# A two-layer kernel on one core: the second layer's up product by seven block products over pairs of batches

## The chip, the core and the metric

One core of a Trainium2 chip. TensorE (PE) does matrix products into PSUM, eight banks of 128 x 512 fp32; VectorE (DVE) and ScalarE (ACT) read PSUM and SBUF and work element by element; GpSimd (POOL) and SyncE (SP) here only issue DMA transfers, each on a queue of its own. The metric is device time of one execution in microseconds; lower is better.

## The reference

```python
attn_out = _attn_ref(x, state)            # x (4, 8, 512, 64), state (4, 8, 32, 64)
x = attn_out.transpose(0, 2, 1, 3).reshape(4 * 544, 512)
h = x @ w_in;  g = h - tanh(h);          x = g @ w_out     # 512 -> 2048 -> 512
h = x @ w2_in; g = h * tanh(softplus(h)); out = g @ w2_out  # 512 -> 2048 -> 512
```

Attention gives per batch 512 rows read by x and 32 read by the states: 4 x 512 rows and 128 state rows. Two layers follow, each an up product (512 to 2048), an elementwise function and a down product (2048 to 512). The weights come as float64.

## The kernel before

Every fp32 product is made of three matmuls on pairs of fp32r tiles (`mm3p`): high x high, high x low, low x high. `split` makes such a pair: a copy to fp32r on ACT or DVE gives the high part, a subtraction on DVE the low part. Weights arrive as float64 by SP, and `conv_steps` turns them into fp32 (two ACT instructions and one on DVE, two after the second layer's table is loaded).

The first layer runs batch after batch (0, 1, 2, state rows, 3), each in 16 steps of 128 columns of d_ff (the state rows in 4 steps). A step has an up product of 6 matmuls, `elem1` (tanh on ACT, subtraction on DVE, a split) and, three steps later (`LA = 3`), a down product of 12 matmuls into four banks. Other work is attached to steps (`at`): attention of the next batch, `sw` (state times weight), and `late_conv`, which converts the second layer's weights along a ramp, and goes on in the second layer's first 13 steps.

The second layer cuts the 17 chunks of 128 rows into blocks of 4, 4, 4, 3 and 2 chunks (`BLOCKS`). `up_2` makes 128 columns of d_ff for a block: 4 k tiles x 3 matmuls, 512, 384 or 256 columns wide; Mish on ACT; a split. `down_2`, three steps later, adds 3 matmuls of 512 columns per chunk, in PSUM over all 16 steps; only the last step is copied out and stored. All split weights of the second layer stay in SBUF.

Buffers are 91 slots of 128 x 512 fp32, handed out oldest first (`get`, `put`); some 1024-wide buffers are given out as halves. In the second layer ACT and DVE work in program order (`Pinned`); in the first, the scheduler chooses it by priority. All instructions on PE, ACT and DVE are recorded under one line, 59, so rows are told apart by their tiles: `h` is an up product, `acc` a down product, `ath`/`swh` first-layer operands, `yh`/`yl` second-layer inputs, `gh`/`gl` the split result of the elementwise function, `wh`/`wl` split weights.

Of the kernel before, what the change touches and what calls it, by code (L numbers as in the profile page):

```python
# [9 lines left out]
F32 = mybir.dt.float32  # L10
# [10 lines left out]
REBIAS = 2.0 ** -112  # L21
NEGATIVE = 2.0 ** 32
PLAIN = 3
YSPARE = 4

# [46 lines left out]
def attention_moe_kernel(  # L72
# [25 lines left out]
        )  # L98

    TE, AC, V = (Pinned(e, order) for e in (nc.tensor, nc.scalar, nc.vector))  # L100
    misc = ctx.enter_context(tc.tile_pool(name="misc", bufs=1))
    small = ctx.enter_context(tc.tile_pool(name="small", bufs=2))
    stage = ctx.enter_context(tc.tile_pool(name="stage", bufs=3))
# [9 lines left out]
    def get(name, dtype=F32, newest=False):  # L113
        if halves and dtype == F32:
            return halves.popleft()
        i = free.pop() if newest else free.popleft()
        return Unit(slots.tile([128, 512], dtype, tag=f"k{i}", name=name), i)

    def put(*units):
        for u in units:  # L120
            if u.slot is None:
                halves.append(u)
            else:
                free.append(u.slot)
# [101 lines left out]
        )  # L226
        return h, l

    W1I, W1O, W2I, W2O = {}, {}, {}, {}

    def conv_w1i(c, k):
        W1I[c, k] = conv32(("w1i", c, k))
# [318 lines left out]
    def acc_bank(i, tags=("a0", "a1", "a2", "a3")):  # L551
        return psum.tile([128, 512], F32, tag=tags[i % len(tags)], name=f"acc{i}")
# [75 lines left out]
        put(u)  # L628
        Y["s"] = y

    chunks = [(b, r) for b in range(3) for r in range(4)] + [("s", 0)] + [(3, r) for r in range(4)]
    blocks = []
    for z in BLOCKS:
        blocks.append(chunks[:z])
        chunks = chunks[z:]

    def y_piece(n):
        ch = blocks[n]
        runs = []
        for i, (b, r) in enumerate(ch):  # L640
            if runs and runs[-1][0] == b:
                runs[-1][3] += 128
            else:
                runs.append([b, r * 128, i * 128, 128])
        k = len(YB.setdefault(n, []))
        yh, yl = get("yh", F32R), get("yl", F32R)
        for b, s0, d0, w in runs:
            src = Y["s"].t[:, k * 128:(k + 1) * 128] if b == "s" else Y[b, k].t[:, s0:s0 + w]
            AC.activation(out=yh.t[:, d0:d0 + w], in_=src, func=ACTF.Copy)
            V.tensor_tensor(  # L650
                out=yl.t[:, d0:d0 + w], in0=src, in1=yh.t[:, d0:d0 + w].bitcast(F32),
                op=ALU.subtract,
            )
        YB[n].append((yh, yl))
        for b, r in ch:
            if b != "s" and r == 3:
                put(Y.pop((b, k)))

    def y_block(n, spare=0):
        if n < len(blocks):  # L660
            while len(YB.get(n, [])) < KD and len(free) >= 2 + spare:
                y_piece(n)
                if spare:
                    break

    ACCT = ["a0", "a1", "a2", "a3"]
    HT = ["s1", "s0", "h0", "h1"]
    acc_n = [0]
    def up_2(n, t):
        N = 128 * len(blocks[n])  # L670
        h = h_bank(HT)[:, :N]
        c, f = t // 4, (t % 4) * 128
        for k in range(KD):
            wh, wl = W2I[c, k]
            yh, yl = YB[n][k]
            mm3p(
                h, wh.t[:, f:f + 128], wl.t[:, f:f + 128], yh.t[:, :N], yl.t[:, :N],
                k == 0, k == KD - 1,
            )
        if t == NT - 1:  # L680
            for p in YB.pop(n):
                put(*p)
        g = get("g")
        AC.activation(out=g.t[:, :N], in_=h, func=ACTF.Mish)
        G["2", n, t] = split(g.t[:, :N], N, "g")
        put(g)

    def down_2(n, t):
        ch = blocks[n]
        if t == 0:  # L690
            ACC["2", n] = []
            for _ in ch:
                ACC["2", n].append(acc_bank(acc_n[0], ACCT))
                acc_n[0] += 1
        gh, gl = G.pop(("2", n, t))
        wh, wl = W2O[(t,)]
        for i, (b, r) in enumerate(ch):
            s = slice(i * 128, (i + 1) * 128)
            acc = ACC["2", n][i]
            if t == NT - 1 and n == len(blocks) - 1 and i == len(ch) - 1:  # L700
                o = get("o")
                rows_out = out[b * T:b * T + S, :].rearrange("(p r) d -> p r d", r=4)[:, r, :]
                for c0, parts in ((0, (256,)), (256, (128, 128))):
                    c1 = c0 + 256
                    mm3p(
                        acc[:, c0:c1], gh.t[:, s], gl.t[:, s], wh.t[:, c0:c1], wl.t[:, c0:c1],
                        False, True, skip_group_check=c0 > 0,
                    )
                    for e, m in enumerate(parts):
                        a = slice(c0 + e * m, c0 + (e + 1) * m)  # L710
                        evac(o.t[:, a], acc[:, a], e)
                    nc.sync.dma_start(out=rows_out[:, c0:c1], in_=o.t[:, c0:c1])
                put(o)
                continue
            mm3p(acc, gh.t[:, s], gl.t[:, s], wh.t, wl.t, t == 0, t == NT - 1)
            if t == NT - 1:
                o = get("o")
                evac(o.t, acc, i)
                if b == "s":
                    for bb in range(B):  # L720
                        nc.sync.dma_start(
                            out=out[bb * T + S:(bb + 1) * T, :], in_=o.t[bb * NS:(bb + 1) * NS, :]
                        )
                else:
                    nc.sync.dma_start(
                        out=out[b * T:b * T + S, :].rearrange("(p r) d -> p r d", r=4)[:, r, :],
                        in_=o.t,
                    )
                put(o)
        put(gh, gl)  # L730


    wi = [
        (("w1i", c, k), cols(w1i, c, k) if c else ftile(w1i, k)) for c in range(4) for k in range(KD)
# [3 lines left out]
        pending.append((("w1o", t), rows(w1o, t)))  # L738
        pending.extend(wi[5 + t:6 + t])
    for c in range(4):  # L740
        for k in range(KD):
            pending.append((("w2i", c, k), cols(w2i, c, k)))
    for t in range(NT):
        pending.append((("w2o", t), rows(w2o, t)))

    side = {}

# [21 lines left out]
    for n in range(len(blocks)):  # L769
        start["2", n] = len(seq)  # L770
        seq += [("2", n, t) for t in range(NT)]

    for s in range(16):
        at(s, lambda s=s: conv_w1o(s))
# [24 lines left out]
    at(start["2"] - 4, lambda: y_block(0))  # L799
    late = [(W2I, ("w2i", i // 4, i % 4)) for i in range(16)]  # L800
    late += [(W2O, ("w2o", i)) for i in range(16)]
    ramp = [
        (start["s"] - 16, 0), (start["s"], 6), (start[3], 10), (start["2"], 25),
        (start["2"] + 13, len(late)),
    ]
    done = [0]

    def late_conv(i):
        for (s0, n0), (s1, n1) in zip(ramp, ramp[1:]):
            if s0 <= i < s1:  # L810
                goal = n0 + (n1 - n0) * (i + 1 - s0) / (s1 - s0)
                while done[0] < goal and len(free) >= (RESERVE if i < start["2"] else 5):
                    conv_split(*late[done[0]])
                    done[0] += 1

    def load_state(g):
# [81 lines left out]
    at(4, lambda: state_t(1, st[1]))  # L898
    banks[2:] = []

    def widen():
        for t in wide:
            put(*(Unit(t[:, h * 512:(h + 1) * 512], None) for h in range(2)))

    at(start[1], widen)
# [1 line left out]
    def up(q):  # L907
        if q[0] == "x":
            up_x(q[1], q[2])
        elif q[0] == "s":  # L910
            up_s(q[1])
        else:
            if q[2] == 0:
                if q[1] == 0:
                    pre = nc.scalar.preload_act_table_set("mish").ins
                    signed[0] = False
                    order(pre, last[0])
                    AC.last, V.last = pre, None
                    AC.floor = V.floor = None
                    AC.on = V.on = True  # L920
                y_block(q[1])
            up_2(*q[1:])

    def down(q):
        if q[0] == "x":
            down_x(q[1], q[2])
        elif q[0] == "s":
            down_s(q[1])
        else:
            down_2(q[1], q[2])  # L930

    def ahead(i):
        return LA if i < len(seq) else 0

    low = 0
    for i in range(len(seq) + 1):
        marks.append([e.recent for e in engines])
        q = seq[i] if i < len(seq) else None
        if q:
            up(q)  # L940
            if q[0] == "2" and q[2] >= NT - 6:
                y_block(q[1] + 1, YSPARE)
        for f in side.pop(i, []):
            f()
        while low < len(seq) and low <= i - ahead(i):
            down(seq[low])
            low += 1
        pinned = AC.on, V.on
        AC.on = V.on = False
        late_conv(i)  # L950
        AC.on, V.on = pinned


# [31 lines left out]
```

## Time and profile before

| | |
|---|---|
| median of 3 runs | 744.0 us (743.06 to 744.3) |
| the profiled execution | 743.11 us, span 741.3 us |
| PE busy | 726.9 us (98%), 4147 matmuls |
| DVE busy | 304.1 us (41%), 533 instructions |
| ACT busy | 332.6 us (45%), 612 instructions |
| POOL busy | 6.6 us (1%) |
| granted clock of PE | 1.00 throughout (2.4 GHz), 0.97 in the last 21 us |
| DMA | 43.1 MB, mean 58 GB/s |

The first layer's last batch begins near 285 us, and the second layer's first up product is issued at 355.3 us. A row of the timeline gives start, duration, engine, line, operation, output <- inputs and count; matmuls overlap, so the time of one is read from the distance of their starts. A table by stage gives busy time and number of instructions per engine.

### The profile page before, as it was taken

Reading aid. Unit: us, or ns where it says so; the run is one execution under the profiler, and the core shown is the slowest. Engines: PE = TensorE matmul, PEld = TensorE weight load, DVE = VectorE, ACT = ScalarE, POOL = GpSimd, SP = SyncE. Lnnn points to the kernel's source line nnn. Section 1 sums busy time; section 2 is a strip of 40 time slices with the busy share of each in tenths; the row PEclk is TensorE's granted clock in tenths of the full one; section 3 lists DMA queues with packets and bytes.
Section 4 is the critical chain, followed back from the end, with each engine's and each line's share of the span. In section 5 each row is a group of like instructions: output and inputs, shape, how many; then the busy total and the mean of one; then the engine's idle time right before and its main releaser. Section 6 shows DMA issues by size and latency. Waiting matters only on the chain.

```text
span 741.3 us, 10004 instructions
## 1 busy us (share of the span) xinstructions
PE 726.9 (98%) x4147; PEld 591.4 (80%) x4147; DVE 304.1 (41%) x533; ACT 332.6 (45%) x612; POOL 6.6 (1%) x14
## 2 busy tenths in 40 slices
PE   8899999999999999999999999999999999999997
PEld 6467877788777898778888888888888888998996
DVE  5899654844456443787633222111221111111111
ACT  6998544544554443787744333122231223223322
POOL 0000010001000000000000000000000000000000
PEclk9999999999999999999999999999999999999999
DMA  9984110003110110453400001000010000100100
GB/s 291 331 301 142 57 57 1 1 2 100 43 29 1 58 57 1 142 171 114 142 28 1 1 0 57 1 0 1 1 57 1 0 1 1 57 0 1 43 1 28
DMA packets 17308, 43.10 MB, mean 58 GB/s; under 512 B 2672, under 2 KB 7024, under 8 KB 17264
## 3 DMA queue, kind: packets, MB, share of 16 engines
q1 hardware_dynamic: 16624, 40.38, 16.3%
q0 software_dynamic: 640, 2.10, 1.0%
q8 instruction: 32, 0.52, 0.3%
q14 instruction: 12, 0.10, 0.1%
HBM read 38.01 MB, written 4.46 MB: 57 GB/s over the span
## 4 chain that ended last, share of the span: by engine, by line
PE 91%; ACT 6%; DVE 2%; DMA 1%; issue 0%; SPq 0%; ACTq 0%
PE acc L59 47%; PE h L59 37%; PE swp L59 2%; ACT w L59 2%; ACT r L59 2%; PE srd L59 1%; PE xtp L59 1%; ACT swh L59 1%; DMA x<-in_x_dram 1%; ACT t L59 1%; PE sct L59 1%; PE atp L59 1%; PE e2p L59 1%; DVE swl L59 0%; PE sc L59 0%
## 5 line engine op out<-in xcount | busy, mean ns | idle before, releaser
L59 DVE TENSOR_TENSOR gl<-wide,gh 128x512 fp32r<-128x512 f32 (+2 forms) x74 | 44.8, 605 | 198.3 <-ACT gh L59 198.3
L59 ACT ACTIVATE wide<-h 128x512 f32<-128x512 f32 (+2 forms) x74 | 39.0, 527 | 187.4 <-PE h L59 182.9
L59 PE MATMUL h<-yh,wl 128*128 128x512 f32 (+2 forms) x320 | 114.4, 358 | 0.0
L59 PE MATMUL h<-yl,wh 128*128 128x512 f32 (+2 forms) x320 | 114.3, 357 | 0.0
L59 PE MATMUL h<-yh,wh 128*128 128x512 f32 (+2 forms) x320 | 114.3, 357 | 0.0
L59 PE MATMUL acc<-wh,gh 128*128 128x512 f32 x289 | 112.7, 390 | 0.6 <-ACT wide L59 0.6
L59 PE MATMUL acc<-wl,gh 128*128 128x512 f32 x289 | 112.7, 390 | 0.0
L59 PE MATMUL acc<-wh,gl 128*128 128x512 f32 x289 | 112.5, 389 | 0.0
L59 PE MATMUL acc<-gh,wh 128*128 128x512 f32 x244 | 99.1, 406 | 0.0
L59 PE MATMUL acc<-gl,wh 128*128 128x512 f32 x244 | 95.4, 391 | 0.0
L59 PE MATMUL acc<-gh,wl 128*128 128x512 f32 x244 | 95.4, 391 | 0.0
L59 PEld LDWEIGHTS h<-yl,wh 128*128 128x128 f32 x320 | 60.2, 188 | 8.9 <-DVE yl L59 0.2
L59 PEld LDWEIGHTS h<-yh,wh 128*128 128x128 f32 x320 | 60.3, 188 | 8.9
L59 PEld LDWEIGHTS h<-yh,wl 128*128 128x128 f32 x320 | 60.3, 188 | 7.5
L59 PEld LDWEIGHTS acc<-wh,gh 128*128 128x128 f32 x289 | 54.3, 188 | 11.9 <-ACT t L59 0.8
L59 PEld LDWEIGHTS acc<-wh,gl 128*128 128x128 f32 x289 | 54.2, 188 | 11.4
L59 PEld LDWEIGHTS acc<-wl,gh 128*128 128x128 f32 x289 | 54.3, 188 | 10.2
L59 PEld LDWEIGHTS acc<-gh,wh 128*128 128x128 f32 x244 | 45.8, 188 | 17.2 <-issue 5.6
L59 DVE TENSOR_TENSOR gl<-g,gh 128x512 fp32r<-128x512 f32 x24 | 16.6, 692 | 94.3 <-ACT gh L59 94.3
L59 PEld LDWEIGHTS acc<-gh,wl 128*128 128x128 f32 x244 | 45.8, 188 | 9.9
L59 PE MATMUL h<-ath,swh 128*128 128x512 f32 x128 | 51.4, 402 | 1.8 <-DVE t L59 1.6
L59 PEld LDWEIGHTS acc<-gl,wh 128*128 128x128 f32 x244 | 45.9, 188 | 9.1 <-issue 0.8
(123 smaller groups left out, 925.6 us busy)
## 6 DMA issues: line engine op xcount, KB each, us to landing
st<-in_moe_w_in_dram SPq DMA_DIRECT2D x27, 512.0 KB, 4.6
st<-in_moe_w_out_dram SPq DMA_DIRECT2D x22, 512.0 KB, 3.4
wide<-in_moe_w_out_dram SPq DMA_DIRECT2D x10, 512.0 KB, 5.1
out_dram<-wide SPq DMA_DIRECT2D x11, 256.0 KB, 2.1
wide<-in_moe_w_in_dram SPq DMA_DIRECT2D x5, 512.0 KB, 6.4
x<-in_x_dram SPq DMA_DIRECT2D x8, 256.0 KB, 5.7
x<-in_x_dram POOLq DMA_DIRECT2D x6, 256.0 KB, 3.2
out_dram<-o SPq DMA_DIRECT2D x4, 256.0 KB, 2.3
```

Source lines behind the costliest of these rows:

```text
L59: i = fn(*args, **kw)
```

## The change

The up product of the second layer is computed for two batches at a time. The 256 columns of d_ff of a *group* (two f tiles) times two batches make 2 x 2 blocks of 128 x 512, and the inner dimension is cut in halves of two k tiles: seven block products (m1 to m7) of sums of weights with sums of inputs, instead of eight. The chunks of the state rows are multiplied the plain way, transposed, beside the second pair. There are two pairs (`u`) x 8 groups (`g`).

The weight sums (forms a1, a2, s12, s34) are made in the first layer in fp32, split, and stored to DRAM by POOL; in the second layer SP loads a group's forms and its part of the down weights, for each pair again. The sums of inputs are made by DVE from the first layer's output and split; those of the second pair in the first pair's groups. Down products of a group run as *fill* between the products of the next group (`slot`); a chunk has 6 matmuls over the group's two f tiles, and DVE adds it to a sum in SBUF. After the last step of the first layer there is no look-ahead of up products any more: the first layer's last three down steps are the fill of the first group.

```diff
-YSPARE = 4
+EARLY = 11
-BLOCKS = [4, 4, 4, 3, 2]
+    def store_split(w, dst):
+        for u, d in zip(split(w.t, name="w"), dst):
+            v = u.t.bitcast(F32)
+            nc.gpsimd.dma_start(out=d, in_=v if len(d.shape) == 2 else v.rearrange("p (g e) -> p g e", g=2))
+            put(u)
+        put(w)
+    def pieces_2i(c, k):
...
+            for o, x, y, op in (
+                (s12[:, :, 0], a1[:, :, 1], a2[:, :, 1], ALU.add),
+                (s12[:, :, 1], s12[:, :, 0], a1[:, :, 0], ALU.subtract),
+                (s34[:, :, 0], a1[:, :, 0], a1[:, :, 1], ALU.subtract),
+                (s34[:, :, 1], a2[:, :, 0], s12[:, :, 1], ALU.subtract),
+            ):
+                V.tensor_tensor(out=o, in0=x, in1=y, op=op)
...
+        return [lambda: conv(0), lambda: conv(1), combine] + [lambda x=x: keep(x) for x in FORMS]
...
+    LEFT = {
+        "m1": ("a1", 0), "m2": ("a2", 0), "m3": ("s34", 1), "m4": ("a2", 1),
+        "m5": ("s12", 0), "m6": ("s12", 1), "m7": ("s34", 0),
+    }
+    RIGHT = {"m1": "b11", "m2": "b21", "m3": "b22", "m4": "t4", "m5": "t1", "m6": "t2", "m7": "t3"}
...
+    def product(u, g, m, bank, start):
+        x, op = LEFT[m]
+        for k in range(KH):
+            yh, yl = YB[u, RIGHT[m], k]
+            mm3p(
+                bank, w2(g, x, k, 0, op), w2(g, x, k, 1, op), yh.t, yl.t,
+                start and k == 0, k == KH - 1, skip_group_check=not start,
+            )
...
+    def mish(key, src, spare=None):
+        u = spare or get("g")
+        AC.activation(out=u.t, in_=src, func=ACTF.Mish)
+        h = get("gh", F32R)
+        AC.activation(out=h.t, in_=u.t, func=ACTF.Copy)
+        return key, u, h
+    def mish_lo(key, u, h):
+        l = get("gl", F32R)
+        V.tensor_tensor(out=l.t, in0=u.t, in1=h.t.bitcast(F32), op=ALU.subtract)
...
+    def down_2(g, b, r, gs, last):
+        d_n[0] += 1
+        ps = psum.tile([128, 512], F32, tag=DB[d_n[0] % len(DB)], name="acc")
...
+        o = OUT[b, r]
+        if g < NT // 2 - 1:
+            V.tensor_tensor(out=o.t, in0=ps, in1=o.t, op=ALU.add)
+            return
...
+    def group(u, g, fill, ahead, with_s, rate):
+        a, b, c = (psum.tile([128, 512], F32, tag=t, name="h") for t in UB)
...
+        def slot():
+            if fill:
+                fill.popleft()()
+            for _ in range(2):
+                if ahead:
+                    ahead.popleft()()
+            background(rate, 0)
...
+        product(u, g, "m1", a, True)
+        m1 = copy_of(a)
+        slot()
+        product(u, g, "m6", b, True)
+        p = plus(b, m1)
+        slot()
+        product(u, g, "m7", c, True)
...
+        slot()
+        product(u, g, "m2", a, False)
+        c11 = mish((0, 0), a)
+        slot()
+        mish_lo(*c11)
...
+        product(u, g, "m5", b, False)
+        q = plus(b, m1)
+        h22 = plus(c, q, q)
+        c22 = mish((1, 1), h22.t, h22)
+        slot()
+        mish_lo(*c22)
+        product(u, g, "m3", b, False)
+        h12 = plus(b, m1, m1)
+        c12 = mish((0, 1), h12.t, h12)
+        slot()
+        mish_lo(*c12)
+        product(u, g, "m4", c, False)
+        h21 = plus(c, p, p)
+        c21 = mish((1, 0), h21.t, h21)
+        slot()
+        mish_lo(*c21)
+        while fill or ahead:
+            slot()
...
+    pace = [(start[1] + 8, 0), (start["s"], 40), (start["2"], 110)]
...
+    fill = [lambda q=q: down(q) for q in seq[low:]]
+    groups = [(u, g) for u in range(2) for g in range(NT // 2)]
+    for j, (u, g) in enumerate(groups):
+        ahead = loads_out(g)
+        if j + 1 < len(groups):
+            ahead += loads_in(g + 1)
...
+        if (u, g) == (0, 1):
+            later = pieces_y(1)
+            bg.extend(pieces_ys() + later[:EARLY])
+        elif (u, g) == (0, NT // 2 - 1):
+            bg.extend(later[EARLY:])
+        group(u, g, fill, ahead, u == 1, 2 if g == NT // 2 - 1 else 1)
+        fill = downs(u, g, u == 1, j + 1 == len(groups))
```

On PE in the second layer, a block of the kernel before: the end of an up product and the beginning of the down step behind it.

```order
L59 MATMUL h<-yh,wh 128x512
L59 MATMUL h<-yl,wh 128x512
L59 MATMUL h<-yh,wl 128x512
L59 MATMUL acc_4236<-wh,gh 128x512
L59 MATMUL acc_4236<-wl,gh 128x512
L59 MATMUL acc_4236<-wh,gl 128x512
L59 MATMUL acc_4237<-wh,gh 128x512
L59 MATMUL acc_4237<-wl,gh 128x512
```

The same place in the changed kernel, one product of a group with its neighbours (`ws` a loaded form, `wo` a loaded down weight):

```order
L58 MATMUL acc<-wo,gh 128x512 x2
L58 MATMUL acc<-wo,gl 128x512
L58 MATMUL acc<-wo,gh 128x512 x2
L58 MATMUL acc<-wo,gl 128x512
L58 MATMUL h<-yh,ws 128x512
L58 MATMUL h<-yl,ws 128x512
L58 MATMUL h<-yh,ws 128x512 x2
L58 MATMUL h<-yl,ws 128x512
L58 MATMUL h<-yh,ws 128x512
L58 MATMUL acc<-wo,gh 128x512 x2
L58 MATMUL acc<-wo,gl 128x512
L58 MATMUL acc<-wo,gh 128x512 x2
L58 MATMUL acc<-wo,gl 128x512
```

Products of 6 matmuls now alternate with down chunks of 6, where an up product of 12 was followed by a whole down step.

On DVE in the second layer, before: the low parts (`gl`), the inputs of the next block (`yl`) and the copies of finished sums.

```order
L59 TENSOR_TENSOR gl<-g,gh 128x512 x5
L59 TENSOR_TENSOR yl<-y,yh 128x512 x4
L59 TENSOR_TENSOR gl<-g,gh 128x512 x3
L59 COPY o<-acc_3659 128x512
L59 COPY o<-acc_3661 128x512
L59 TENSOR_TENSOR gl<-g,gh 128x512 x8
```

In the changed kernel, a group of the second pair from p on (`wide<-h` the sums of products p, q and those behind them, `gl<-gt` the state rows, `wide<-acc` the down sums):

```order
L58 TENSOR_TENSOR wide<-h,wide 128x512
L58 TENSOR_TENSOR wide<-acc,wide 128x512 x3
L58 TENSOR_TENSOR gl<-g,gh 128x512
L58 TENSOR_TENSOR gl<-gt,gh 128x256
L58 TENSOR_TENSOR wide<-h,wide 128x512 x2
L58 TENSOR_TENSOR wide<-acc,wide 128x512
L58 TENSOR_TENSOR gl<-wide,gh 128x512
L58 TENSOR_TENSOR wide<-h,wide 128x512
L58 TENSOR_TENSOR wide<-acc,wide 128x512
L58 TENSOR_TENSOR gl<-wide,gh 128x512
L58 TENSOR_TENSOR wide<-h,wide 128x512
L58 TENSOR_TENSOR wide<-acc,wide 128x512
L58 TENSOR_TENSOR gl<-wide,gh 128x512
```

DVE has the sums of products and of down chunks beside the low parts, in this fixed order.

On SP, before, at the end of the weight loads:

```order
L187 DMA st<-in_moe_w_out_dram 128x1024 x2
L187 DMA st<-in_moe_w_in_dram 128x1024 x16
L187 DMA st<-in_moe_w_out_dram 128x1024 x16
L725 DMA out_dram<-o 128x512 x4
L725 DMA out_dram<-wide 128x512 x8
```

In the changed kernel, at the same place:

```order
L187 DMA st<-in_moe_w_in_dram 128x1024 x4
L187 DMA st<-in_moe_w_out_dram 128x1024 x4
L749 DMA ws<-wi 128x512 x8
L756 DMA wo<-wo 128x512 x4
L749 DMA ws<-wi 128x512 x7
L756 DMA wo<-wo 128x512
```

After the float64 weights SP issues the loads of the forms, group by group.

## Rows read from the trace of the kernel before

**Rows 1.** Page, part 1: the span and PE's busy time.

```profile
span 741.3 us, 10004 instructions
...
PE 726.9 (98%) x4147; PEld 591.4 (80%) x4147; DVE 304.1 (41%) x533; ACT 332.6 (45%) x612; POOL 6.6 (1%) x14
```

**Rows 2.** Busy time by stage: stretch, then us and instructions per engine, clock, DMA share, GB/s.

```profile
40.00:80.00 40.00, 38.44 (x186) 28.23 (x185) 37.34 (x67) 33.98 (x61) 0.00 (x0) 1.00 0.56 190
94.00:168.80 74.80, 73.64 (x574) 57.40 (x573) 42.23 (x88) 35.72 (x67) 2.07 (x3) 1.00 0.06 17
168.80:268.00 99.20, 98.17 (x653) 78.23 (x653) 49.94 (x87) 46.58 (x83) 2.88 (x4) 1.00 0.15 44
268.00:355.30 87.30, 86.64 (x509) 69.85 (x507) 56.77 (x88) 59.64 (x107) 0.00 (x0) 1.00 0.32 103
463.00:560.00 97.00, 97.00 (x429) 80.32 (x429) 16.22 (x24) 24.49 (x41) 0.00 (x0) 1.00 0.03 11
```

**Rows 3.** Grouped rows by shape: matmuls of the second layer.

```profile
L59 PE MATMUL h<-yh,wh 128*128 128x512 f32 x192 | 74.7, 389 | 0.0
...
L59 PE MATMUL h<-yh,wh 128*128 128x384 f32 x64 | 21.6, 337 | 0.0
...
L59 PE MATMUL h<-yh,wh 128*128 128x256 f32 x64 | 18.0, 282 | 0.0
...
L59 PE MATMUL acc<-wh,gh 128*128 128x512 f32 x287 | 112.1, 390 | 0.0
```

**Rows 4.** Timeline of PE: start, us, then the instruction; first and last of runs.

```profile
469.64 0.39 PE L59 MATMUL h<-yh,wh 128*128 128x512 f32 x1
...
472.36 0.39 PE L59 MATMUL acc<-wh,gh 128*128 128x512 f32 x1
...
643.68 0.33 PE L59 MATMUL h<-yh,wh 128*128 128x384 f32 x1
...
644.91 0.33 PE L59 MATMUL h<-yl,wh 128*128 128x384 f32 x1
...
701.68 0.28 PE L59 MATMUL h<-yh,wh 128*128 128x256 f32 x1
...
703.12 0.40 PE L59 MATMUL acc<-wh,gh 128*128 128x512 f32 x1
...
267.42 1.04 PE L59 MATMUL atp<-ident,a 128*128 128x128 f32 x8
268.21 0.48 PE L59 MATMUL acc<-gh,wh 128*128 128x512 f32 x1
```

**Rows 5.** Timeline of ACT and DVE behind an up product.

```profile
472.56 0.60 ACT L59 ACTIVATE g<-h 128x512 f32<-128x512 f32 x1 [4.18 <-PE h L59]
...
473.19 0.63 ACT L59 ACTIVATE gh<-g 128x512 fp32r<-128x512 f32 x1
...
473.85 0.69 DVE L59 TENSOR_TENSOR gl<-g,gh 128x512 fp32r<-128x512 f32 x1 [4.75 <-ACT gh L59]
```

**Rows 6.** Timeline of POOL and DVE: x loads issued, and DVE pairs.

```profile
71.77 1.28 DVE L59 TENSOR_TENSOR wl<-w,wh 128x512 fp32r<-128x512 f32 x2
...
93.63 1.29 DVE L59 TENSOR_TENSOR wl<-w,wh 128x512 fp32r<-128x512 f32 x2
...
93.91 1.44 POOL L271 DMA_DIRECT2D x<-in_x_dram  x2 [1.84 <-PE acc L59]
```

**Rows 7.** Timeline of the end of the span.

```profile
736.10 0.28 PE L59 MATMUL acc<-wh,gh 128*128 128x256 f32 x1
...
737.23 0.38 PE L59 MATMUL acc<-wh,gh 128*128 128x256 f32 x1 [0.61 <-ACT wide L59]
...
738.19 0.29 DVE L59 COPY wide<-acc 128x128 f32<-128x128 f32 x1 [5.38 <-ACT wide L59]
```

**Rows 8.** DMA issues: count, KB each, median us to landing.

```profile
x<-in_x_dram POOLq DMA_DIRECT2D x6, 256.0 KB, 3.2
...
st<-in_moe_w_in_dram SPq DMA_DIRECT2D x27, 512.0 KB, 4.6
```

More of the change, by code (lines that the diff above doesn't have):

```diff
@@ L629, in state_y @@
         Y["s"] = y
[L631 to L642, printed above, removed]
-            else:
[L644 to L730, printed above, removed]
@@ new lines, in pieces_ys, with keep, background, load_group @@
+    def pieces_ys():
+        def keep():
+            YB["s"] = split(Y["s"].t, name="y")
+            put(Y.pop("s"))
+        return [keep]
+    bg = deque()
+    def background(n, spare):
+        while n > 0 and bg and len(free) >= spare:
+            bg.popleft()()
+            n -= 1
+    UB = ["h0", "h1", "s0"]
+    DB = ["a0", "a1", "a2"]
+    SB_, TB = "s1", "a3"
+    W2, O2, G2, OUT = {}, {}, {}, {}
+    def load_group(g, x, k):
+        W2[g, x, k] = u = get("ws", F32R)
+        nc.sync.dma_start(
+            out=u.t.bitcast(F32).rearrange("p (h e) -> p h e", h=2), in_=D2I[g // 2, x, k][g % 2]
+        )
@@ new lines, in s_up @@
+    def s_up(g, bank):
+        ys_h, ys_l = YB["s"]
+        for kk in range(KD):
+            x, k = ("a1", "a2")[kk // KH], kk % KH
+            wv = W2[g, x, k].t.rearrange("p (h e) -> p h e", h=2)
+            c = slice(kk * 128, (kk + 1) * 128)
+            mm3p(
+                bank[:, :256], ys_h.t[:, c], ys_l.t[:, c], wv[:, 0], wv[:, 1],
+                kk == 0, kk == KD - 1,
+            )
+        u = get("gs")
+        AC.activation(out=u.t[:, :256], in_=bank[:, :256], func=ACTF.Mish)
+        return u
@@ new lines, in s_turn @@
+    def s_turn(g, u, bank):
+        for f in range(2):
+            TE.transpose(
+                out=bank[:, f * 128:(f + 1) * 128], in_=u.t[:, f * 128:(f + 1) * 128],
+                identity=ident,
+            )
+        put(u)
+        G2["s"] = split(bank[:, :256], 256, name="g")
+    def mish(key, src, spare=None):
[4 more added lines that the diff above has]
+        return key, u, h
@@ new lines, in downs, with one @@
+    def downs(u, g, with_s, last=False):
+        gs = {k: G2.pop(k) for k in list(G2)}
+        order = [(2 * u + 1, r) for r in range(4)]
+        order += [("s", 0)] if with_s else []
+        order += [(2 * u, r) for r in range(4)]
+        done = []
+        def one(i):
+            down_2(g, *order[i], gs, last and i == len(order) - 1)
+            done.append(i)
+            if len(done) == len(order):
+                for x in gs.values():
+                    put(*x)
+                put(*O2.pop(2 * g), *O2.pop(2 * g + 1))
+        return [lambda i=i: one(i) for i in range(len(order))]
@@ L733, in attention_moe_kernel, with loads_in, loads_out @@
+    def loads_in(g):
+        g %= NT // 2
+        return deque(
+            [lambda x=x, k=k: load_group(g, x, k) for x in ("a1", "s12", "s34", "a2") for k in range(KH)]
+        )
+    def loads_out(g):
+        return deque([lambda t=t: load_out(t) for t in (2 * g, 2 * g + 1)])
     wi = [
@@ L740, in attention_moe_kernel @@
     for c in range(4):
[L741 to L744, printed above, removed]
+        for k in range(KH):
+            for j in (k, k + KH):
+                pending.append((("w2i", c, j), cols(w2i, c, j)))
+            bg.extend(pieces_2i(c, k))
+        for t in range(4 * c, 4 * c + 4):
+            pending.append((("w2o", t), rows(w2o, t)))
+            bg.extend(pieces_2o(t))
     side = {}
@@ L909, in up @@
             up_x(q[1], q[2])
-        elif q[0] == "s":
+        else:
             up_s(q[1])
[L912 to L922, printed above, removed]
     def down(q):
@@ L926, in down @@
             down_x(q[1], q[2])
-        elif q[0] == "s":
+        else:
             down_s(q[1])
[L929 to L933, printed above, removed]
     low = 0
-    for i in range(len(seq) + 1):
+    for i, q in enumerate(seq):
         marks.append([e.recent for e in engines])
[L938 to L942, printed above, removed]
+        up(q)
         for f in side.pop(i, []):
             f()
-        while low < len(seq) and low <= i - ahead(i):
+        while low <= i - LA:
             down(seq[low])
             low += 1
[L948 to L951, printed above, removed]
+        keep_pace(i)
+    pre = nc.scalar.preload_act_table_set("mish").ins
+    signed[0] = False
+    order(pre, last[0])
+    for e in engines:
+        e.last, e.floor, e.on = None, None, True
+    AC.last = pre
+    widen(stage.tile([128, 1024], F32, tag="st", name="wide") for _ in range(3))
+    for f in loads_in(0):
+        f()
+    fill = [lambda q=q: down(q) for q in seq[low:]]
[4 more added lines that the diff above has]
+            ahead += loads_in(g + 1)
+        if g == 0:
+            background(len(bg), 0)
+        if (u, g) == (0, 1):
[5 more added lines that the diff above has]
+        fill = downs(u, g, u == 1, j + 1 == len(groups))
+    for f in fill:
+        f()
 _INS = ["x", "state", "moe_w_in", "moe_w_out", "moe2_w_in", "moe2_w_out"]
```

139 lines of the change are left out of this document (122 added, 17 removed).

## The prediction

> **What bounds the kernel now.** I read the page's first part and the tables by stage first: the span is 741.3 us and TensorE (PE) is busy in 726.9 of it [rows 1]. By stages [rows 2] PE is busy in all 97.00 of 97.00 us of the second layer, where VectorE (DVE) works 16 and ScalarE (ACT) 24 us, and in 86.6 of the 87.3 us of the last batch of the first layer, where DVE and ACT work 57 and 60. So in the second layer only PE's own instruction stream counts, and what leaves that stream leaves the span, as long as DVE, ACT and the DMA queues keep up. That stream has a fixed pitch, which the timeline shows between issues [rows 4]: 512 columns 0.2267 us (12 issues from 469.64 to 472.36), 384 columns 0.176 (7 from 643.68 to 644.91), 256 columns 0.120 (12 from 701.68 to 703.12), a 128-column transpose 0.099 (8 from 267.42 to 268.21). The means of 0.39 us in the grouped rows are overlapped and no price.
>
> **The change, part by part.**
> *Up product.* Before, each of the three kinds of matmul counts 192 of 512 columns, 64 of 384 and 64 of 256 [rows 3], so 576 x 0.2267 + 192 x 0.176 + 192 x 0.120 = 130.6 + 33.8 + 23.0 = 187.4 us. After, two pairs of batches x 8 groups x 7 products x 2 k tiles x 3 = 672 matmuls of 512 columns = 152.3 us; the state rows cannot be paired and take 8 x 12 of 256 columns = 11.5 us and 16 transposes = 1.6 us. Sum 165.4: 22.0 us less. The down product keeps 17 chunks x 16 tiles x 3 = 816 matmuls (272 of each kind; the other 16 of the 287 whole ones and the one in halves in [rows 3] are the first layer's state rows), 185.0 us on both sides. Per group PE now has 42 + 48 = 90 matmuls, 20.4 us, in the first pair, and 96 + 12 + 2, 23.4 us, in the second.
>
> *Chain in a group.* Product m5 leaves its bank to m3, but first DVE must read the bank (q); one down chunk, 6 x 0.2267 = 1.36 us, stands between the two products. From [rows 4, 5], ACT starts 0.20 us after the next issue behind a product (472.36 to 472.56), the copy follows 0.63 later, DVE's low part 0.66 after that and takes 0.69. So q ends at 0.20 + 0.69 = 0.89, 0.37 to 0.47 us before m3 must issue, if DVE is free. Queued ahead of q on DVE stand the low part of the first tile (mish begins 0.20 after m2, low part ends 1.98 after that, 0.5 us before m5 ends) and, in the second pair, a 256-column piece of the state rows, which ends about 0.3 after m5; q then ends near 1.0 and still fits. Behind q wait the second sum, the next down sum and its low part; only the next group's down chunks need these, 4 us later. I price an ordinary group at nothing: 17 DVE instructions x 0.69 = 11.7 us in 20.4. The adds of the down sums (136 chunk adds where 17 evacuations stood) lie in that sum, and three rotating banks give each 2.7 us.
> It is not so in the first group: it has only the 3 left-over downs of the first layer as fill, so nothing stands between m5 and m3. There DVE ends the low part 0.82 after m5, q at 1.51, and m3 waits 1.6 us; then the sums and low parts follow on DVE and ACT in turn, 2.2 for the second sum, 4.3 for its low part, 5.0 for the third sum, 7.0 for its low part, which the first down chunk of group 1 needs. PE gets there at 5.7 (1.6 + 3 x 1.36), waits to 6.35 for the high part and then some 0.3 for the low one: 1.0 us. Together +2.6. In the three groups that carry background work (the pieces of the second pair's right-hand forms) one or two splits stand ahead of q, 0.2 to 0.6 us each time: +1.5 in all (bounds 0 and 6, if three waits per group show).
>
> *First layer.* The conversions of the second layer's weights move before the second layer, with 16 more splits, 32 half-size DVE sums, and 22 full DVE instructions and 14 splits for the first right-hand forms. By the order of the built program the last batch goes from 88 to 127 DVE and from 107 to 118 ACT instructions, that is 58 and 54 per 40 us. The nearest row is the stretch 40 to 80 us [rows 2]: 67 and 61 instructions, DVE busy 37.3 of 40 us, and PE still busy 38.4. So such a density costs up to 1.6 us in 40. Back to back two DVE instructions take 1.28, that is 0.60 and 0.68 [rows 6], so 127 want some 76 of the 87 us. I take +1.5, near that row; bounds 0 and 15 (with no overlap 127 x 0.69 = 87.6 us, and 15 more if DVE, which waits for ACT in turn, is busy for only 85% of the time).
>
> *Stores and loads.* 48 splits go to DRAM as 96 stores on POOL's queue; POOL issues two transfers of the same shape in 1.44 us [rows 6], so 69 us of the some 225 between the middle of the second batch (131 us) and 355 us, at no cost as long as slots come back. In the second layer a group loads 12 x 256 KB on SP's queue: 3.15 MB per 20.4 us, 154 GB/s. In 40 to 80 us the chip moved 190 GB/s at a DMA share of 0.56 [rows 2], so the stream should fit in half the capacity; loads are issued about a group ahead. Cost 0.
> The Trainium skill, "DMA: Bandwidth & Descriptors", section Bandwidth, asks for transfers of 1 MiB or more and gives (for GpSimd's queue) 138 GB/s for 64 KB and 341 for 1 MB; transfers of 256 KB lie between, and at its lower figure a group of the first pair would take 22.8 us, 2.4 more than PE, an estimate of some 19 us over 8 groups. The row of 190 GB/s comes from 512 KB transfers, so it does not settle 256 KB ones.
> The Trainium skill, "GPSIMD Engine Reference", section 1. Specifications, says that GpSimd shares SBUF interfaces with VectorE and that two SBUF inputs contend, which the added sums and low parts all have. Here POOL's two issues at 93.91 take 0.72 each and DVE's pair beside them 1.29 against 1.28 without POOL [rows 6]: no contention in this trace, so the sum stays; a doubled issue would bring the stores to 138 of 225 us.
>
> *End.* Before, the last chunk is cut in halves and waits 0.61 for an evacuation [rows 7]; now it is one piece, then two half adds (about 0.42 each). From the end of the last product's issue it then takes 0.2 + 0.8 + 2.8 (from the last evacuation's end, 738.48, to 741.3) = 3.8 us, against 741.3 - 736.8 = 4.5 (six half matmuls from 736.10 on, unwaited): -0.6, bounds -1 and +1.
>
> *Sum.* -22.0 + 2.6 + 1.5 + 1.5 - 0.6 = -17.0 us: span 724.3. The profiled execution took 743.1, 1.8 over its span, and the median of the runs is 744.0, so 726 to 727; I say 727.
>
> **Rivals.**
> A. The chain shows in every group: DVE or ACT reach q 0.3 to 0.9 us late, so 16 groups lose 5 to 14 us: 732 to 741. For: the margin is only 0.4 us, and DVE's order is fixed. Against: DVE has over 8 us idle per group (20.4 - 11.7).
> B. The first layer stretches by 6 to 15 us, since main chain and conversions alternate on two engines and share the buffer halves: 731 to 740. Against: the 40 to 80 us stretch.
> C. Slower: slots wait for stores. All 96 stand in one in-order queue on POOL beside batch 3's loads of x; the low parts' slots are given out again only when a store has landed, and tanh of the main path takes such slots. A transfer there lands 3.2 us after issue [rows 8]; one after another 96 x 3.2 = 307 us, 82 over the 225: 727 + 82 = 809 at worst, slower from 2.5 us a store on. Against: two issues in 1.44 us, and 20 to 45 free slots.
> D. The weight stream binds, slower than before from about 1.8 us for each of the twelve transfers of a group. If they land one behind the other at 3.2 us [rows 8], a group takes 38.4 us, 8 x 18.0 + 8 x 15.0 = 264 us more than PE wants: 991; with two in flight it is hidden. Against: 512 KB land in 4.6 us with others in flight [rows 8]. By the page on DMA above it would be 727 + 19 = 746.
> E. All is hidden but the first group: -22.0 + 2.6 - 0.6, 723 to 724.
>
> **How the numbers follow.** Forecast with E, 721 to 732: 0.65. A: 0.15. B: 0.08. C: 0.05. D: 0.04, the rest 0.03 near no change. 0.2% (1.5 us) is about what a measurement of this kernel can tell from no change. Faster: forecast, A and B, 0.87 after a bit of A and B is lost to the middle; same 0.04; slower 0.09, from C and D. The range 720 to 738 leaves out C, D and the ends of A and B; the likeliest case's own is 721 to 732.
>
> **What would show it.** Right: PE's issue pitch in groups stays 0.2267; one gap of about 1.6 us before m3 of the first group and one of about 1 us in the second; the second layer from its first product to the last takes some 364 us against 382; the first layer ends within 3 us of 355. Wrong: waits of h matmuls for DVE in every group (A); the first product later than 360 us (B, C), with ACT or DVE waiting for DMA (C); waits of PE for DMA on ws or wo tiles (D).

## The result, and the profile after

The changed kernel takes 747.9 us (median of 5 runs, 746.74 to 749.81) against 743.1 us (742.73 to 744.3) for the kernel before on the same chip: a ratio of 1.0062 with the interval 1.0043 to 1.0082. It is slower by 0.6%, where 727 us were predicted. The profiled execution took 747.16 us.

The page's first part, to be set against [rows 1]:

```profile
span 745.4 us, 10557 instructions
...
PE 716.6 (96%) x3968; PEld 572.9 (77%) x3968; DVE 463.7 (62%) x787; ACT 352.9 (47%) x631; POOL 70.4 (9%) x110
```

PE has 179 matmuls fewer and is busy 10.3 us less, yet the span is 4.1 us longer. So PE now waits somewhere. The place shows when four points of both traces are laid side by side: the start of the instruction `ath` on ACT for batches 1, 2 and 3, and the second layer's first product.

| | batch 1 | batch 2 | batch 3 | first product | from batch 1 to first product | from there to the end |
|---|---|---|---|---|---|---|
| before | 91.1 | 167.2 | 268.1 | 355.3 | 264.2 | 386.0 |
| after | 90.7 | 173.6 | 279.5 | 377.7 | 287.0 | 367.6 |

The first product of the second layer, before and then after:

```profile
355.33 0.39 PE L59 MATMUL h<-yh,wh 128*128 128x512 f32 x1
```

```profile
377.75 0.39 PE L58 MATMUL h<-yh,ws 128*128 128x512 f32 x1
```

The second layer is 18.4 us shorter, and the first, from batch 1 on, 22.8 us longer: 6.8 us between the first two points, 5.0 between the next two and 11.0 after the start of batch 3 (the state rows lie across that start). All that PE waits for from 370 us to the end is this (the waits of PE: what waited <- for what, us in total, times, longest):

```profile
PE h L58 <- DVE wide L58: 1.9, 2, 1.5
PE acc L58 <- ACT gh L58: 0.3, 1, 0.3
```

These are 2.2 us of waits in the second layer, and no product or chunk waits for a load of `ws` or `wo`. The first layer is read by stretches, in the columns of [rows 2]:

```profile
40.00:80.00 40.00, 38.41 (x187) 28.32 (x187) 36.96 (x66) 33.62 (x60) 0.00 (x0) 1.00 0.55 189
...
165.00:175.00 10.00, 9.02 (x139) 8.54 (x139) 5.55 (x11) 4.92 (x9) 2.18 (x3) 0.56 0.47 165
175.00:268.00 93.00, 90.83 (x589) 70.96 (x588) 59.90 (x108) 54.09 (x97) 24.66 (x37) 0.99 0.49 164
268.00:310.00 42.00, 42.00 (x319) 36.07 (x318) 27.83 (x47) 26.53 (x47) 14.87 (x22) 1.00 0.65 218
310.00:320.00 10.00, 6.29 (x19) 4.80 (x19) 5.82 (x9) 7.32 (x13) 2.16 (x4) 0.66 0.83 283
320.00:350.00 30.00, 30.00 (x155) 22.96 (x154) 23.16 (x41) 20.89 (x39) 13.78 (x20) 1.00 0.85 286
350.00:360.00 10.00, 5.19 (x14) 3.79 (x13) 8.29 (x14) 7.98 (x15) 2.46 (x5) 0.70 0.74 254
```

Most stretches have PE full. Three stretches of 10 us do not, and in those the granted clock is 0.56, 0.66 and 0.70. In the three, DVE and ACT are not full either: somebody waits for something else. The last of the three holes, on PE's timeline (start, us, instruction, in brackets the idle time before it and who ended it):

```profile
350.13 0.39 PE L58 MATMUL acc<-gh,wl 128*128 128x512 f32 x1
355.33 0.79 PE L58 MATMUL h<-ath,swh 128*128 128x512 f32 x1 [4.81 <-DVE wide L58]
355.92 0.63 PE L58 MATMUL h<-atl,swh 128*128 128x512 f32 x1
...
360.61 0.51 PE L58 MATMUL acc<-gh,wh 128*128 128x512 f32 x1
360.96 0.40 PE L58 MATMUL acc<-gl,wh 128*128 128x512 f32 x1
```

Two losses follow each other here. PE stands still for 4.81 us. Then it runs at the half clock (1.2 instead of 2.4 GHz): from 355.92 to 360.61 the 11 distances are 0.426 us each where [rows 4] have 0.2267, so 2.2 us more. What PE waited for was a DVE instruction at 354.59. Behind that stands ACT's timeline in the same stretch:

```profile
344.13 0.62 ACT L58 ACTIVATE gh<-wide 128x512 fp32r<-128x512 f32 x1
347.65 0.63 ACT L58 ACTIVATE yh<-wide 128x512 fp32r<-128x512 f32 x1 [2.90 <-DMA wo<-wh]
348.19 0.66 ACT L58 ACTIVATE wide<-st 128x512 uint32<-128x512 uint32 x1
...
350.88 0.57 ACT L58 ACTIVATE t<-h 128x512 f32<-128x512 f32 x1
...
353.57 0.58 ACT L58 ACTIVATE wide<-h 128x512 f32<-128x512 f32 x1
```

`yh<-wide` splits a right-hand form, which nobody needs before the second layer. It stood in ACT's stream ahead of its turn, and its slot was still being stored to DRAM: ACT waited 2.90 us for that store to land. Ten instructions then ran back to back before `wide<-h`, the tanh that PE's next bank hung on. The waits of ACT for DMA that sum to over 2 us, from 94 to 380 us:

```profile
ACT r L58 <- DMA st<-in_moe_w_in_dram: 7.4, 4, 3.0
...
ACT r L58 <- DMA wo<-wh: 5.2, 1, 5.2
...
ACT yh L58 <- DMA wo<-wh: 2.9, 1, 2.9
ACT e L58 <- DMA wi<-wh: 2.9, 1, 2.9
...
ACT w L58 <- DMA wi<-wh: 2.3, 1, 2.3
ACT r L58 <- DMA st<-in_moe_w_out_dram: 2.1, 1, 2.1
```

`wo<-wh` and `wi<-wh` are stores: the instruction got a slot whose store had not landed. `st<-` are loads of float64 weights. Not every such wait makes a hole: behind the longest, 5.2 us at 191.1, PE had none. The first hole (164.91, 2.60 us, and 166.78, 0.98 us) follows on the `w` and `e` waits, the second (314.37, 3.71 us) on the wait for `in_moe_w_out`, a load and not a slot. With a smaller one at 240.27 (1.74 us, 0.63 before), the holes are 12.5 us longer than before, and the half-clock stretches cost some 9.7 us: 4.4 round 165 to 176.7, 2.6 and 2.7 behind the other two. Together 22.2, of 22.8.

### The profile page after: what moved, and what is told of

The parts are those of the page before. It is cut to its first block, busy times and chain, and to the rows that moved or that the text cites. A ratio compares the mean times of both kernels' runs of the same rounds, so it can differ in the third digit from the quotient of the medians.

```text
span 745.4 us, 10557 instructions
## 1 busy us (share of the span) xinstructions
PE 716.6 (96%) x3968; PEld 572.9 (77%) x3968; DVE 463.7 (62%) x787; ACT 352.9 (47%) x631; POOL 70.4 (9%) x110
## 3 DMA queue, kind: packets, MB, share of 16 engines
q0 software_dynamic: 8320, 27.27, 10.3%
## 4 chain that ended last, share of the span: by engine, by line
PE 63%; issue 15%; ACT 7%; POOL 5%; DMA 5%; DVE 4%; SPq 1%; POOLq 0%; DVEq 0%; ACTq 0%
PE acc L58 34%; PE h L58 24%; POOL wi L241 4%; ACT r L58 2%; ACT w L58 2%; PE hs L58 2%; DMA wi<-wh 1%; POOL wo L241 1%; DMA wi<-wl 1%; DMA x<-in_x_dram 1%; ACT gh L58 1%; DVE wide L58 1%; DVE gl L58 1%; PE srd L58 1%; ACT wide L58 1%
## 5 line engine op out<-in xcount | busy, mean ns | idle before, releaser
L58 PE MATMUL acc<-wo,gh 128*128 128x512 f32 x544 | 168.0, 390 | 0.3 <-ACT gh L58 0.3
L58 PE MATMUL h<-yh,ws 128*128 128x512 f32 x448 | 156.9, 392 | 2.0 <-DVE wide L58 1.9
L58 DVE TENSOR_TENSOR wide<-acc,wide 128x512 f32<-128x512 f32 (+1 forms) x106 | 72.4, 685 | 80.9 <-PE acc L58 79.7
L58 PEld LDWEIGHTS acc<-wo,gh 128*128 128x128 f32 x544 | 101.5, 188 | 21.5 <-ACT gh L58 0.8
L58 PE MATMUL acc<-wo,gl 128*128 128x512 f32 x272 | 105.9, 389 | 0.0
L58 PEld LDWEIGHTS h<-yh,ws 128*128 128x128 f32 x448 | 84.1, 188 | 20.9 <-DVE wide L58 3.6
L58 PE MATMUL h<-yl,ws 128*128 128x512 f32 x224 | 87.4, 390 | 0.0
L58 DVE TENSOR_TENSOR wide<-h,wide 128x512 f32<-128x512 f32 x89 | 61.2, 688 | 31.3 <-ACT wide L58 17.8
L58 PEld LDWEIGHTS acc<-gh,wh 128*128 128x128 f32 x244 | 46.9, 192 | 17.5 <-issue 6.4
L58 PEld LDWEIGHTS acc<-wo,gl 128*128 128x128 f32 x272 | 51.1, 188 | 11.2 <-DVE gl L58 0.4
L58 PE MATMUL h<-ath,swl 128*128 128x512 f32 x128 | 50.9, 398 | 0.1
```

The lines of the kernel that those rows point to most:

```text
L58: i = fn(*args, **kw)
```

## The experiments

Theory S (slots): the stores hold slots until they land, and the main chain gets such slots. Theory O (order): the instructions of the background work (conversions, sums, right-hand forms) are put into ACT's and DVE's streams ahead of the step they are written in; there they wait, and the main chain behind them waits too. Theory T (traffic): POOL's stores slow the weight loads. Theory D (density): DVE and ACT simply have more to do. A run's table row is read from its one profiled execution, its time is the median; in e13 the two lie apart (744.9 us profiled, median 749.7). The runs were made on several chips, on which the kernel before took 743.1 (beside after) to 744.5 us, so differences of a microsecond between runs are better read from the ratios.

| run | time, us | ratio to before | batch 1 | batch 2 | batch 3 | first product | first layer | second layer |
|---|---|---|---|---|---|---|---|---|
| e1_fixed_tile | 767.7 | 1.029 to 1.035 | 132.3 | 208.5 | 311.7 | 399.4 | 267.1 | 367.1 |
| e2_no_stores | 737.8 | 0.989 to 0.994 | 91.8 | 174.9 | 280.0 | 370.1 | 278.3 | 367.0 |
| e3_held | 733.3 | 0.983 to 0.987 | 94.0 | 170.1 | 274.9 | 367.8 | 273.8 | 367.4 |
| e4_reserve20 | 760.9 | 1.019 to 1.025 | 91.0 | 167.0 | 278.7 | 389.7 | 298.7 | 367.1 |
| e6_held_pace | 741.6 | 0.993 to 0.998 | 93.6 | 174.9 | 284.8 | 373.6 | 280.0 | 367.1 |
| e8_held_fill | 731.5 | 0.982 to 0.985 | 93.1 | 169.1 | 272.5 | 364.6 | 271.5 | 365.4 |
| e9_held_late | 736.6 | 0.987 to 0.991 | 92.2 | 168.3 | 271.9 | 362.6 | 270.4 | 372.1 |
| e10_late_pace | 743.8 | 0.996 to 1.001 | 90.4 | 170.4 | 279.9 | 368.9 | 278.5 | 369.7 |
| e11_held_fill_nost | 727.6 | 0.974 to 0.980 | 92.3 | 168.4 | 270.5 | 361.2 | 268.9 | 364.7 |
| e12_held_act | 731.0 | 0.981 to 0.986 | 93.6 | 169.6 | 274.4 | 365.4 | 271.8 | 367.3 |
| e13_held_dve | 749.7 | 1.005 to 1.009 | 93.7 | 172.8 | 277.2 | 376.1 | 282.4 | 367.0 |
| e14_held_act_fill | 728.7 | 0.979 to 0.983 | 90.9 | 167.0 | 270.0 | 360.4 | 269.5 | 364.6 |

### Stores without their slots

```diff
-            v = u.t.bitcast(F32)
+            v = zero
...
```

(e1_fixed_tile: all stores write one fixed tile, so the second layer's weights are zero; one slot fewer.)

> All 96 stores are issued as before, but read one fixed tile, so no buffer slot has to wait until a store has landed (the forms in DRAM are then zeros; one slot fewer). Theory S (ACT, in order, stands before instructions whose slot a store still reads, and PE runs dry): the holes of PE at 164.9 (2.6 and 1.0 us) and 355.3 (4.8) go with their half-clock stretches, the second layer's first product comes near 366 instead of 377.7, the time near 736. Theory T (the traffic of the stores delays the weight loads): the first product stays near 377. Theory D (ACT and DVE are simply too full): also unchanged, 746 to 748.

It missed, by a flaw of the edit: the stores no longer depended on anything, so POOL issued them at the very start, on top of the first weight loads (PE, its clock, DMA share, GB/s in the columns of [rows 2]):

```profile
20.00:60.00 40.00, 26.32 (x167) 15.87 (x168) 17.31 (x36) 20.72 (x41) 21.40 (x33) 0.70 1.03 407
60.00:100.00 40.00, 33.47 (x148) 22.46 (x146) 26.82 (x47) 29.48 (x52) 19.64 (x30) 0.96 1.02 414
```

What can be used is the rest: from batch 1 on, with no store left in that stretch, the first layer takes 267.1 us. Without stores, 20 of the 22.8 us are gone, and the clock from 132 to 399 us is 1.00. That speaks for S, O or T, and leaves 2.9 us for D.

### Ten stores of 96

```diff
-            nc.gpsimd.dma_start(out=d, in_=v if len(d.shape) == 2 else ...)
+            if d is not None:
+                nc.gpsimd.dma_start(out=d, in_=v if d is None or len(d.shape) == 2 else ...)
...
```

(e2_no_stores: only the first forms and the first down weight are stored, and all loads of the second layer read these.)

> 10 of the 96 stores remain; all groups load the same forms, so the loads of the second layer are as many and as large (the products are then of wrong weights). Theory S and T together: neither slots nor weight loads wait for stores, all three holes go, the first product comes within 3 us of 356, the time is 725 to 729. Theory D: the first layer keeps most of its 22 us, 740 or more.

10 us came back, less than S and T together forecast and more than D alone. Eight of the ten stores that stayed are the earliest, and the hole at the end of batch 1 stayed with them (2.97 and 0.98 us):

```profile
ACT r L58 <- DMA st<-in_moe_w_in_dram: 5.3, 4, 1.9
...
ACT r L58 <- DMA st<-in_moe_w_out_dram: 2.9, 1, 2.9
...
ACT w L58 <- DMA wi<-wh: 2.8, 1, 2.8
ACT e L58 <- DMA wi<-wh: 2.7, 1, 2.7
```

The `w` and `e` instructions wait there for stores to land, so at that place it is the slot: S. It does not rule out traffic, as the eight stores run close together there (194 GB/s from 150 to 167 us). The waits for weight loads are still there without stores, so T is not their cause alone.

### More slots kept free

```diff
-RESERVE = 10
+RESERVE = 20
```

(Background work starts only while 20 slots are free.)

> Background pieces run only while 20 slots are free instead of 10. Theory S for the first hole (3 to 13 free slots at the end of the second batch, so a freed slot is handed out again before its store has landed): the hole at 164.9 goes, the third batch begins 5 to 6 us earlier. But the pieces move into the last batch, which is the fullest: there it may cost more; 742 to 750.

The first hole is gone (batch 2 begins at 167.0, as before): that the free slots were too few there is shown. But the pieces pile up behind it, the time is above the forecast, and the waits come back larger round the start of batch 3, on PE:

```profile
282.44 1.96 PE L58 MATMUL swp<-w,sbt 64*32 64x128 f32 x64 [8.74 <-DVE atl L58]
289.91 1.96 PE L58 MATMUL swp<-w,sbt 64*32 64x512 f32 x16 [5.51 <-DVE swl L58]
```

### Pieces held to their step, and on which engine

```diff
+                kept = [e.floor for e in engines]
+                AC.floor, V.floor = marks[-1][1:]
                 while done[0] < goal and bg and len(free) >= RESERVE:
                     bg.popleft()()
                     done[0] += 1
+                for e, m in zip(engines, kept):
+                    e.floor = m
```

(e3_held: an instruction of a piece may not be put ahead of the instructions recorded before the present step. In e12_held_act only `AC.floor` is set, in e13_held_dve only `V.floor`.)

> The background pieces may not be placed ahead of the step in whose turn they are written (on ACT and DVE). If the wait at 344.8 to 347.7 comes from a split of a right-hand form that the scheduler put ahead of its turn, onto a slot whose store had just been issued, that hole goes (some 7 us with its half-clock stretch), 739 to 742. If the order is not the point, 746 to 749; if held pieces delay the main path, longer.

> Background pieces may not be put ahead of their step on ScalarE; on VectorE they still may. Theory A (what costs is ScalarE's in-order stream: a piece put ahead of its step waits there for a slot or a weight load, and the main chain behind it waits too): most of the 14.6 us that holding both engines gave comes back, 733 to 738, and the waits of ScalarE for DMA over 2 us go. Theory V (it is VectorE's stream, where the low parts and sums of the pieces stand ahead of the main chain's): 743 to 749, no gain.

> The reverse: pieces are held to their step on VectorE only. Theory A (ScalarE's stream costs): 743 to 749, with the ScalarE waits for DMA still there. Theory V (VectorE's stream): 733 to 738. If both engines' streams are needed for the gain, this and the run that holds ScalarE alone each land between 738 and 744.

Holding both gains 14.6 us, more than expected, as the first hole went too. Holding ACT alone gains as much (731.0), holding DVE alone nothing (749.7); in after DVE waits for no DMA at all from 94 to 380 us. The waits of ACT for DMA over 1.5 us with ACT held:

```profile
ACT r L58 <- DMA st<-in_moe_w_in_dram: 3.0, 1, 3.0
...
ACT w L58 <- DMA wi<-wl: 2.4, 2, 1.6
...
ACT r L58 <- DMA wi<-wl: 1.6, 1, 1.6
```

One wait over 2 us is left, for a weight load, where none was forecast. And with DVE held, where the hole before the last step is the old one:

```profile
ACT r L58 <- DMA wo<-wh: 3.6, 1, 3.6
...
ACT yh L58 <- DMA wo<-wh: 3.0, 1, 3.0
...
ACT e L58 <- DMA wi<-wh: 2.1, 1, 2.1
...
354.29 0.79 PE L58 MATMUL h<-ath,swh 128*128 128x512 f32 x1 [4.92 <-DVE wide L58]
```

So it is ACT's stream: a background instruction ahead of its turn waits there for a slot in store or for a weight load, and the main chain stands behind it. O and S are one mechanism: the same stores with a later place in the stream cost little. T is not needed for it. With ACT held the weight loads from 150 to 375 us land even later after their issue than in after (medians 5.1 and 5.5 us for `in_moe_w_out` and `in_moe_w_in`, against 4.5 and 5.1; 3.8 and 4.1 in e2), and yet 15 us of the first layer are back.

### Where the pieces go

```diff
-    pace = [(start[1] + 8, 0), (start["s"], 40), (start["2"], 110)]
+    pace = [(start[1] + 8, 0), (start["s"], 50), (start["2"], 110)]
```

(e6_held_pace: e3 with 50 pieces due before the state rows. e9_held_late: e3 with 101 due at the end, and the last eight right-hand splits in the first group. e10_late_pace: both.)

> As e3, with 50 instead of 40 pieces due before the state rows, so that the third batch carries more and the last less. Theory D (what is left of the stretch is fullness of the last batch): the last batch gets shorter than e3's 92.9 us by 2 to 4 and the time is 729 to 732. Theory S (few free slots in the third batch): the third batch gets longer by as much or more, 732 to 740.

> As e3, with the last 8 splits of the first pair's right-hand forms in the first group's slots, where ACT and DVE are nearly idle, instead of in the last batch. Theory D: 8 instructions less on ACT and on DVE there make the last batch 3 to 5 us shorter, 728 to 731. If fullness is not what is left: unchanged, 732 to 735. If they come late for m2, m5, m3 or m4: a wait of PE in the first group.

> e9 and the pace of e6 together. If both help, 726 to 729; if the pace costs in the third batch, as e6 against e3.

Earlier pieces win 4.1 us in batch 3 (88.8 against 92.9 us in e3) and lose 5.2 in batch 1 and 5.1 in batch 2; in batch 2 again ACT meets a slot in store, and PE stands still over the same time (ACT, then PE):

```profile
206.25 0.63 ACT L58 ACTIVATE wh<-wide 128x512 fp32r<-128x512 f32 x1 [2.64 <-DMA wo<-wh]
```

```profile
208.78 1.11 PE L58 MATMUL xtp<-ident,wide 128*128 128x128 f32 x4 [5.46 <-DVE swl L58]
```

Later pieces win 3.4 us in the first layer and lose 4.7 in the second: PE waits 2.62 us for the first product and 3.13 before m3. The two together (e10, 743.8) are no better than either. Held pieces thus still wait when their step itself comes too early, and PE waits when it comes too late.

### The first group's fill

```diff
-    fill = [lambda q=q: down(q) for q in seq[low:]]
+    fill = [lambda: None] * 3 + [lambda q=q: down(q) for q in seq[low:]]
```

(e8_held_fill: e3 with the three left-over down steps after m2, m5 and m3 instead of after m1, m6 and m7. e14_held_act_fill: the same with ACT held alone.)

> As e3, with the first layer's last three down steps as fill behind m2, m5 and m3 of the first group instead of behind m1, m6 and m7. If the reading of the chain in a group is right (nothing between m5 and m3 is what makes PE wait), the gaps of 1.3 to 1.5 us before m3 and of 0.3 before the next group's first down chunk go, and 0.3 may come back before m6: 1.2 to 1.6 us less than e3.

> Both edits that helped, in their smallest form: pieces held to their step on ScalarE alone (731.0), and the three left-over down steps moved behind the products m2, m5 and m3 of the first group, whose waits of 1.47 and 0.30 us they should cover. If the two are independent: 728.5 to 730, the first layer as long as with ScalarE held alone (first anchor to first product 271.8). If the wait before m3 is only moved elsewhere, as the earlier pair of such runs leaves open (731.45 against 733.28): 730.5 to 731.5.

Both waits of the first group are gone in both, and the second layer is 2.0 us (365.4 against 367.4) and 2.7 us (364.6 against 367.3) shorter. e14 is the fastest of those that compute the kernel's own output: 728.7 us, 1.9% under the kernel before and, by the two ratios, 2.5% under the changed one (0.981 / 1.0062). Its profiled execution (span 725.0) is the fastest of its five runs; by stretches:

```profile
310.00:320.00 10.00, 10.00 (x56) 7.37 (x55) 9.04 (x17) 7.93 (x16) 6.79 (x10) 1.00 0.86 304
320.00:350.00 30.00, 27.54 (x131) 21.11 (x131) 25.28 (x43) 20.92 (x38) 10.15 (x16) 1.00 0.96 328
350.00:360.00 10.00, 9.68 (x43) 7.70 (x41) 10.00 (x18) 9.26 (x17) 0.00 (x0) 1.00 0.77 246
```

The clock is 1.00 throughout, and from 310 to 360 us PE is full but for 2.8 us (2.46 of them in 320 to 350).

### What is left

(e11_held_fill_nost: e8 with the ten stores of e2; the second layer reads the same few forms.)

> Leaves out 86 of the 96 stores and lets all loads of the second layer read the same few forms, so its output is not the kernel's; otherwise like the run with held pieces and the three down steps moved (731.45, of which the first layer from the first to the last anchor is still 7.5 us longer than before: 271.5 against 264.0). Theory D (what is left is the number of instructions that DVE and ACT have to do beside the main chain): nothing changes but the loads' latency, 729.5 to 732. Theory H (what is left is still slots held by stores and loads delayed by them): the first layer comes back to within 2 us of before, 724 to 726.

It lies between: 727.6, 3.9 us under e8, and the first layer 268.9 us, 2.6 under e8 and still 4.7 over the 264.2 of before. Its waits of ACT for DMA are 1.3 us in all, so the 4.7 us are not slots or loads. By exclusion they are D, with a hole of 2.09 us behind DVE at 338.52 and a half clock after it; e1 left 2.9. So D is 3 to 5 us. What the stores still hold in e8 is not measured as well: e12 and e14 differ by 2.3 us up to the first product, where their code is the same (271.8 and 269.5), and e14 lies only 0.6 over e11.

## Why the prediction was wrong

**The second layer was right.** Its counts are there: 448 + 224 matmuls of 512 columns in products, 96 of 256, 544 + 272 in chunks. From the first product to the end it takes 18.4 us less, where -22.0 + 2.6 + 1.5 - 0.6 says 18.5. That it comes so close is in part luck, as the terms within it differ: the first group's waits are 1.47 before m3 and 0.33 before the first chunk (2.6 was the term), the groups with background work lose nothing (1.5), one wait of 0.47 opens the second pair, and the end takes 4.2 us from the last issue's end, not 3.8. Some 1.7 us more are spread over the stretch and not named. Rival A is out: of waits for DVE there are only the two that the row of 1.9 us above sums up. The larger:

```profile
394.34 0.50 PE L58 MATMUL h<-yh,ws 128*128 128x512 f32 x1 [1.47 <-DVE wide L58]
```

**The weight stream was right.** The DMA issues of after, in the columns of [rows 8]:

```profile
ws<-wi SPq DMA_DIRECT2D x128, 256.0 KB, 3.6
...
wi<-wh POOLq DMA_DIRECT2D x32, 256.0 KB, 4.2
```

From 420 to 560 us the chip moves 173 GB/s with a DMA share of 0.53 and no wait of PE for it; rival D is out. The estimate that stood beside the Trainium skill's "DMA: Bandwidth & Descriptors", section Bandwidth, some 19 us, does not show: at 256 KB the stream is hidden.

**POOL's own time was right.** It is busy 70.4 us (69 for the stores was the term). A store issue takes 0.72 us beside busy DVE, and DVE's instruction with two inputs keeps its 0.68 to 0.69 beside it (two back to back took 1.28 in [rows 6]); so what the Trainium skill says in "GPSIMD Engine Reference", section 1. Specifications, of contention with two SBUF inputs does not show here either (POOL, then DVE):

```profile
339.20 0.72 POOL L241 DMA_DIRECT2D wi<-wl  x1
```

```profile
339.28 0.68 DVE L58 TENSOR_TENSOR yl<-wide,yh 128x512 fp32r<-128x512 f32 x1
```

**The step that failed is the first layer's "+1.5", with "bounds 0 and 15".** It measured +22.8, past the upper bound, and with that the whole miss of the span (745.4 against 724.3) is named. The sum counted the instructions that DVE and ACT have to do and set them against a stretch of like density, 40 to 80 us. Its counts for the last batch were right (128 on DVE and 120 on ACT after 279.5, for 127 and 118), and density itself cost 3 to 5 us (e1, e11), more than 1.5 but within the bounds. Two things it left out. It looked at the last batch alone, and 11.8 us of the loss lie before it. And it did not count waits: in the 40 to 80 us of the kernel before no slot is held by a store, and the sum did not ask what an instruction that the built order puts ahead of its step waits for there. The 15 to 17.5 us between after (287.0) and the runs with ACT held alone (271.8 in e12, 269.5 in e14) come from background instructions on ACT ahead of their turn, and go when these alone are held to their step; in after they show as holes, and as the half clock behind the holes, for which the sum had no term at all.

**Rival C had half of the mechanism and the wrong size.** It said that the low parts' slots are given out again only when a store has landed, and that tanh of the main path takes such slots; ACT waiting for DMA and a first product past 360 us were named as its signs, and both are there. That background instructions, put early on ACT, would take such slots and hold up the chain behind them, it did not say. Its price took all 96 stores in one queue at 3.2 us each, and its chance of 0.05 rested on "20 to 45 free slots", which e4 disproves for the end of batch 1: asking for 20 would have changed nothing there. A few late slots are enough: in after one wait of ACT of 2.90 us stands ahead of the hole of 4.81 us and its half clock. Rival B's two engines in turn are the 3 to 5 us of e1 and e11, under its 6 to 15.

## What to carry to other kernels

When background work with DMA behind it is mixed into a tuned stream, count per engine not only its instructions but what each of them waits for, and look up in the order of the built program what stands behind it. Hold such work to its step on the engine that the main chain runs through (here one bound on ACT, worth 17 us), and give a waiting place (here the first group) work that is already ready. A short hole in PE costs more than itself if the clock falls behind it: price both.

## What the hardware showed

- After a hole PE often runs at the lower clock (1.2 instead of 2.4 GHz): distances of 0.426 us for 512 columns instead of 0.2267, for some 5 us behind the second and the third hole of after. Not every hole brings it. In e12 and e14 the same matmul waits 2.00 and 2.02 us at the same place; the one is followed, 1.3 us after PE starts again, by 3.4 us at the half clock (granted clock 0.50 from 344.6 to 348.0), the other by none. Why is open.

```profile
343.28 0.50 PE L58 MATMUL h<-ath,swh 128*128 128x512 f32 x1 [2.00 <-DVE wide L58]
...
344.91 0.63 PE L58 MATMUL acc<-gh,wh 128*128 128x512 f32 x1
```

```profile
338.98 0.50 PE L58 MATMUL h<-ath,swh 128*128 128x512 f32 x1 [2.02 <-DVE wide L58]
...
340.70 0.39 PE L58 MATMUL acc<-gl,wh 128*128 128x512 f32 x1
```

- A store of 256 KB from POOL lands 4.1 to 4.6 us after its issue, where the loads of x of the same size in [rows 8] took 3.2. For so long a slot stays out of use after the store is issued.
